# Linear attention and token/channel MLP on one core: q, k and v held as runs of nine tokens, with the head's parity on the partition halves

## The chip, the cores and the metric

The kernel runs on one core of one Trainium2 chip. The metric is the device time of one execution in microseconds (us), the median of several runs. For the kernel before it is 371.67 us (12 runs, 370.39 to 373.3).

## The reference

Inputs are q, k, v of shape (batch 8, heads 8, tokens 576, head width 64), all fp32, and the weights of a token-mixing and a channel MLP.

```python
kv  = einsum('bhsd,bhse->bhde', k, v)          # 64 x 64 for each batch and head
out = einsum('bhsd,bhde->bhse', q, kv)
x   = out / sqrt(mean(out*out, -1) + 1e-6) * g_norm   # heads side by side: (8, 576, 512)
tok = einsum('ts,bsd->btd', w_tok, alpha1*x + beta1)  # w_tok is 576 x 576
u   = x + lam * tok
ch  = relu((alpha2*u + beta2) @ w_ch1) @ w_ch2        # 512 -> 2048 -> 512
result = u + lam * ch                                 # fp32
```

## The kernel before, in words

**A recorded program and a planner.** The kernel does not issue instructions as it is written. `P.op` records an operation with its engine (or a choice of engines), an estimated cost and the keys it reads and writes. `schedule` then lays all operations out in time by those costs, and so fixes the order of each engine's instructions and the PSUM banks; `synchronize` sets the semaphores. On the chip each engine runs its list strictly in the order thus fixed. On SP's queue the early loads have a hand-written order (`order`, line 1059). Before the first channel matmuls of batch 0 the planner fills TensorE's idle time with throw-away matmuls on zeros ("warm", line 1304).

**Layout of q, k, v.** One load (line 494) brings tokens 0 to 511 of one of q, k, v for a batch: four consecutive tokens on each of 128 partitions, for all heads, in pieces of 1024 bytes. Tokens 512 to 575 come by a second load (line 504), one token on each of 64 partitions, in pieces of 256 bytes. The loads of batch 0 are cut in two halves of four heads.

**k^T v** (`kv_groups`, line 589). For each head five matmuls in fp32 accumulate over the token chunks, four chunks of 128 tokens and the tail (its other 64 partitions are zeros, memset at line 1091). Output is 64 x 64; two heads go to the two column halves of the TensorE array (tiles of 128 rows by 64 columns). Each such fp32 matmul stands as two weight loads and two matmuls in the trace, so a batch has 80 of each.

**q times kv.** Batches 0 and 1 take q transposed by TensorE (`qt_groups`, lines 551 and 556) as fp32r: two token chunks lie under each other in 128 partitions (`qtr`), and `kvr` is block-diagonal (line 675; line 680 for the tail). Batches 2 to 7 split q into two bf16 parts (`split_q`, line 529), transpose them by DMA (`qt_dma`, line 536, five transposes of 128 x 1024 elements a batch) and multiply with a two-part bf16 `kvd` (lines 665 and 385).

**The rest.** Norm (lines 706 to 737: square on ScalarE, sums and scaling on VectorE, products with alpha1*lam*g and g on VectorE or GpSimd); token mixing (line 763, tails 776; for batch 0 in two halves, line 797); `a2b` (748) and its transpose into `a2t` (by TensorE at line 868 for batch 1, by DMA at line 860 later; line 829 for batch 0); the first channel matmul with ReLU (898 for even batches, 913 for odd ones, 929 for the first piece of batch 0, eviction at 887 and 888); the second channel matmul (963), the residual add (974) and the store (977, tails 981). Tail tokens of an even and an odd batch share one 128-partition tile.

**The order of the batches.** While batch b runs its channel matmuls, batch b+1 does q times kv and the token mixing, and batch b+2 is loaded, split, transposed, and has its k^T v done among the last matmuls of line 963. Weights w_tok, w_ch1 and w_ch2 are loaded once, between the loads of batches 0 and 1, and cast (w_tok: `wt_groups`, transposes at 1121 and 1138; w_ch1 at 1217; w_ch2 at 1230 and 1235).

Of the kernel before, what the change touches and what calls it, by code (L numbers as in the profile page):

```python
# [14 lines left out]
NH = 8  # L15
S = 576
DH = 64
# [374 lines left out]
def bass_transnormer_attn__then__resmlp_affine_kernel(  # L392
# [15 lines left out]
    with ExitStack() as stack:  # L408
# [5 lines left out]
        with nc.sbuf_tensor("qtr", [128, 20, 128], F32R) as qtr:  # L414
            pass
        qs = sb("qs", [128, 5, NH, 2, DH], BF16)
# [12 lines left out]
        kf = sb("kf", [128, NH, 4, DH], F32)  # L429
        vf = sb("vf", [128, NH, 4, DH], F32)  # L430
        qf = sb("qf", [128, NH, 4, DH], F32)
        kft = sb("kft", [128, NH, DH], F32)
        qft = sb("qft", [128, NH, DH], F32)
        vft = sb("vft", [128, NH, DH], F32)
        with nc.sbuf_tensor("kvr", [128, NH, 128], F32R) as kvr:
            pass
        qt = sb("qt", [128, NH, TP], BF16)
# [54 lines left out]
        def load_main(n, b, hs, at=None):  # L492
            tile, src = {"k": (kf, k), "v": (vf, v), "q": (qf, q)}[n]
            P.op("SP", 0.6, lambda e: e.dma_start(  # L494
                tile[:, hs].rearrange("p h c d -> p h (c d)"),
                src[b, hs, 0:512, :].rearrange("h (p c) d -> p h (c d)", c=4)),
                w=[(n + "f", a) for a in halves(hs)],
                dma_us=3.0 * (hs.stop - hs.start) / 8, at=at,
                slack=0.0 if at is not None else SLACK)

        def load_tail(n, b, hs=ALL[0], at=None):
            tile, src, lo, key = {"k": (kft, k, 0, "kft"), "v": (vft, v, 0, "vft"),
                                  "q": (qft, q, 64 * (b % 2), "qft%d" % (b % 2))}[n]
            P.op("SP", 0.7, lambda e: e.dma_start(  # L504
                tile[lo:lo + 64, hs, :], src[b, hs, 512:576, :].rearrange("h s d -> s h d")),
                w=[(key, a) for a in halves(hs)], dma_us=1.2 * (hs.stop - hs.start) / 8,
                at=at, slack=0.0 if at is not None else SLACK)

        def load_kv(b, at=None):
            for n in "kv":  # L510
                load_main(n, b, ALL[0], at and at(n))
                load_tail(n, b, ALL[0], at and at(n + "t"))

        def load_q(b, at=None):
            load_main("q", b, ALL[0], at and at("q"))
            load_tail("q", b, ALL[0], at and at("qt"))

        def split_q(b):

            lo_, par = 64 * (b % 2), b % 2  # L520
            for c in range(5):
                rows = slice(0, 128) if c < 4 else slice(lo_, lo_ + 64)
                src = qf[:, :, c, :] if c < 4 else qft[rows]
                hi, lo = qs[rows, c, :, 0, :], qs[rows, c, :, 1, :]
                kin = [("qf", 0), ("qf", 1)] if c < 4 else [("qft%d" % par, a) for a in range(2)]
                kh, kl = ((("qs", c, i) if c < 4 else ("qs", c, par, i)) for i in range(2))
                P.op("ACT", act_us(512), lambda e, hi=hi, src=src: copy(e, hi, src),
                     r=kin, w=[kh])
                P.op(dve_pool(512), 0, lambda e, hi=hi, lo=lo, src=src: e.tensor_tensor(  # L529
                    out=lo, in0=src, in1=hi, op=ALU.subtract), r=kin + [kh], w=[kl], port=True)  # L530

        def qt_dma(b):
            for c in range(5):
                keys = ([("qs", c, i) for i in range(2)] if c < 4 else
                        [("qs", c, par, i) for par in range(2) for i in range(2)])
                P.op("SP", 1.3, lambda e, c=c: e.dma_start_transpose(
                    qt[:, :, 128 * c:128 * c + 128],
                    qs[:, c].rearrange("p h i d -> p (h i d)")), r=keys, w=[("qt", c)],
                    dma_us=0.8, slack=SLACK)

        def qt_groups(b):

            def group(a, cp):
                t = P.ptile(1)
                lo = 64 * (b % 2)
                n = 512 if cp < 2 else 128

                def f(e):
                    for i in range(4 if cp < 2 else 2):
                        if cp < 2:  # L550
                            m = e.transpose(t.flat()[:, 128 * i:128 * i + 128],
                                            qf[:, 4 * a + i, 2 * cp:2 * cp + 2, :].rearrange(
                                                "p c d -> p (c d)"), ident[:])
                        else:
                            h = 4 * a + 2 * i
                            m = e.transpose(t.flat()[:, 64 * i:64 * i + 64],
                                            flat(qft[lo:lo + 64, h:h + 2, :]),
                                            ident[lo:lo + 64, lo:lo + 64])
                    return m
                P.op("PE", 0.131 * (4 if cp < 2 else 2), f, cold=True,  # L560
                     r=["ident", ("qf", a) if cp < 2 else ("qft%d" % (b % 2), a)], w=[t])
                if cp < 2:
                    o = qtr[:, 8 * cp + 4 * a:8 * cp + 4 * a + 4, :].rearrange("p h s -> p (h s)")
                    s = lambda: t.flat()
                else:
                    o = qtr[:, 16 + 2 * a:18 + 2 * a, lo:lo + 64]
                    s = lambda: t.flat()[:, 0:128].rearrange("p (h s) -> p h s", h=2)
                P.op(act_dve(n) if b else "ACT", act_us(n), lambda e: copy(e, o, s()),
                     r=[t], w=[("qtr", a, cp)])
            for a in range(2):  # L570
                for cp in range(3):
                    yield lambda a=a, cp=cp: group(a, cp)

        def kv_groups(b, parts=ALL):
            def group(hs):
                t = P.ptile(1)
                h0, np_ = hs.start, (hs.stop - hs.start) // 2
                aa = halves(hs)

                def mm(prs):  # L580
                    def f(e):
                        for pr in prs:
                            for c in range(5):
                                for y in range(2):
                                    h = h0 + 2 * pr + y
                                    o = t.flat(slice(64 * y, 64 * y + 64))[:, 64 * pr:64 * pr + 64]
                                    a, w = ((kf[:, h, c], vf[:, h, c]) if c < 4 else
                                            (kft[:, h], vft[:, h]))
                                    m = e.matmul(o, a, w, start=(c == 0), stop=(c == 4),  # L589
                                                 tile_position=(0, 64 * y))  # L590
                        return m
                    P.op("PE", 0.2 + 0.585 * len(prs), f, cold=True, w=[t, ("kvp", hs.start)],
                         r=[("kf", a) for a in aa] + [("vf", a) for a in aa] + [
                             (n, a) for n in ("kft", "vft") for a in aa] + ["kv0"])
                mm(range(np_))

                def src(h):
                    return t.flat(slice(64 * h, 64 * h + 64))[:, 0:64 * np_].rearrange(
                        "p (x y) -> p x y", y=64)
                if b < R32:  # L600
                    prev = {}
                    for k_, (hp, r_) in enumerate(((0, 0), (1, 0), (1, 1), (0, 1))):
                        o = kvr[64 * r_:64 * r_ + 64, h0 + hp:hs.stop:2,
                                64 * r_:64 * r_ + 64]
                        prev[hp] = [P.op(
                            "ACT" if k_ % 2 == 0 else "DVE",
                            act_us(64 * np_) if k_ % 2 == 0 else dve_us(64 * np_),
                            lambda e, o=o, hp=hp: copy(e, o, src(hp)), hold=[t],
                            r=[("kvp", hs.start), "kvz"], w=[("kvr", a, hp, r_) for a in aa],
                            after=prev.get(hp, []))]  # L610
                    return
                kv5 = kvd[:].rearrange("p (x h) i d -> p x h i d", h=2)
                for h in range(2):
                    for r_ in range(2):
                        hi = kv5[64 * r_:64 * r_ + 64, :, h, 0]
                        P.op("ACT", act_us(256), lambda e, h=h, hi=hi: e.activation(  # L616
                            hi, src(h), ACT.Identity), r=[t], w=[("kvd", h, r_, 0)])
                for h in range(2):
                    for r_ in range(2):
                        rows = slice(64 * r_, 64 * r_ + 64)  # L620
# [720 lines left out]
```

## Time and profile before

| What | Value |
|---|---|
| median of 12 runs | 371.67 us |
| the profiled execution | 373.3 us, of which 371.5 us span from first to last instruction |
| TensorE matmuls busy | 358.3 us, 96% of the span |
| VectorE, ScalarE, GpSimd busy | 57%, 39%, 31% |
| granted TensorE clock, mean | 0.995 |
| DMA | 59.89 MB in 94626 packets, mean 161 GB/s |

Times of the page are in us unless marked ns. PE is TensorE's matmuls, PEld its weight loads, DVE is VectorE, ACT ScalarE, POOL GpSimd, SP SyncE, which issues most DMAs ("SPq"). A row of the groups names line, engine, operation, output<-inputs, shapes and count, then busy time and mean ns of one, then the idle time of the engine before them and what ended it. "busy" of matmuls includes their pipeline, so overlapping ones count once. The chain of waits is followed back from the last instruction.

### The profile page before, as it was taken

To read this page: it belongs to the slowest core of one execution; us is meant where nothing else is said; L and a number is where in the kernel's file an instruction comes from. 1 tells how busy PE (TensorE), PEld (TensorE's weight loads), DVE (VectorE), ACT (ScalarE), POOL (GpSimd) and SP (SyncE) were. 2 spreads that over 40 slices of the span, in tenths; PEclk is the share of its full clock that TensorE was granted. 3 is DMA by queue.
4 is the path that set the end of the run, shared out by engine and by line. 5 is a ranking of instruction groups with operands and counts; after the bars stand their busy time and mean duration, and the time that the engine had idled before them with its cause. 6 is when DMAs were issued, how large, how long until landed. Compare 5 with 4: busy or idle time off the path is not lost.

```text
span 371.5 us, 6839 instructions
## 1 busy us (share of the span) xinstructions
PE 358.3 (96%) x2994; PEld 215.2 (58%) x2787; DVE 210.7 (57%) x315; ACT 145.4 (39%) x250; POOL 115.7 (31%) x91
## 2 busy tenths in 40 slices
PE   8989889999999999999999999999999999999996
PEld 6867557447764465347764564447754554447644
DVE  3446558986388259852867159753854179720021
ACT  1667326226763058104761048306630057007600
POOL 4259115661076006710554003820531004400000
PEclk9999989999999999999999999999999999999999
DMA  7999999809993999269992779146915110230022
GB/s 203 283 346 276 296 328 321 205 19 170 253 241 70 220 284 226 59 136 267 226 196 43 241 210 215 42 115 172 226 29 114 58 30 0 58 99 30 0 58 85
DMA packets 94626, 59.89 MB, mean 161 GB/s; under 512 B 60592, under 2 KB 85444, under 8 KB 94596
## 3 DMA queue, kind: packets, MB, share of 16 engines
q1 hardware_dynamic: 94512, 59.44, 65.8%
q8 instruction: 23, 0.38, 0.4%
q14 instruction: 7, 0.06, 0.0%
q10 hardware_dynamic: 84, 0.02, 0.0%
HBM read 38.60 MB, written 9.44 MB: 129 GB/s over the span
## 4 chain that ended last, share of the span: by engine, by line
PE 82%; DMA 7%; SPq 4%; DVE 3%; POOL 2%; issue 1%; ACT 0%; POOLq 0%; DVEq 0%
PE ps L963 32%; PE ps L913 19%; PE ps L898 12%; PE ps L763 8%; PE ps L589 4%; DMA stg<-in_moe_w_ch_dram 4%; DMA g_bc<-in_g_norm_dram 3%; PE ps L665 2%; PE ps L385 2%; SPq L504 2%; PE ps L776 1%; SPq L494 1%; POOL xm L737 1%; PE ps L675 1%; DVE w L1235 1%
## 5 line engine op out<-in xcount | busy, mean ns | idle before, releaser
L963 PE MATMUL ps<-w,ht 128*128 128x512 bf16 (+1 forms) x569 | 125.8, 373 | 2.0 <-issue 1.1
L963 PEld LDWEIGHTS ps<-w,ht 128*128 128x128 bf16 x592 | 56.8, 98 | 64.4 <-issue 1.2
L887 ACT ACTIVATE ht<-ps,bias 128x640 bf16<-128x640 f32 (+2 forms) x98 | 72.2, 739 | 52.0 <-PE ps L913 39.9
L913 PE MATMUL ps<-a2t,w 128*128 128x320 bf16 x512 | 71.8, 299 | 0.0
L913 PEld LDWEIGHTS ps<-a2t,w 128*128 128x128 bf16 x512 | 49.4, 98 | 19.9
L737 POOL TENSOR_TENSOR xm<-xm,g_bc 128x1024 f32<-128x1024 f32 (+1 forms) x16 | 34.6, 2161 | 68.6 <-DVE rt L734 64.4
L898 PE MATMUL ps<-a2t,w 128*128 128x512 bf16 x231 | 53.8, 381 | 0.8 <-issue 0.3
L974 DVE TENSOR_TENSOR xm<-ps,xm 128x512 f32<-128x512 f32 (+1 forms) x33 | 22.2, 673 | 53.7 <-PE ps L963 53.6
L616 ACT ACTIVATE kvd<-ps 64x256 bf16<-64x256 f32 x24 | 9.1, 378 | 97.9 <-PE ps L589 97.7
L898 PEld LDWEIGHTS ps<-a2t,w 128*128 128x128 bf16 x240 | 22.6, 98 | 25.6 <-issue 0.6
L888 DVE TENSOR_SCALAR ht<-ps,bias 128x512 bf16<-128x512 f32 (+2 forms) x34 | 25.2, 750 | 16.5 <-PE ps L913 9.7
L708 DVE TENSOR_REDUCE small<-sq 128x16 f32<-128x1024 f32 (+3 forms) x27 | 24.9, 931 | 12.8 <-ACT sq L706 12.5
L763 PE MATMUL ps<-rt,wt 128*128 128x512 bf16 x140 | 31.4, 379 | 0.8 <-DVE rt L734 0.8
L529 POOL TENSOR_TENSOR qs<-qf,qs 128x512 bf16<-128x512 f32 x13 | 16.1, 1236 | 46.3 <-ACT qs L481 45.8
L734 POOL TENSOR_TENSOR rt<-xm,e_bc 128x1024 bf16<-128x1024 f32 (+1 forms) x9 | 16.9, 1875 | 41.8 <-DVE xm L730 39.8
L746 DVE TENSOR_TENSOR xm<-ps,xm 128x512 f32<-128x512 f32 x28 | 19.1, 689 | 12.2 <-PE ps L763 11.8
L706 ACT ACTIVATE sq<-ps 128x1024 f32<-128x1024 f32 (+3 forms) x27 | 21.4, 797 | 11.4 <-PE ps L385 8.2
L763 PEld LDWEIGHTS ps<-rt,wt 128*128 128x128 bf16 x140 | 13.6, 98 | 17.6 <-DVE rt L734 1.3
L974 DVE TENSOR_TENSOR xtl<-ps,xtl 128x512 f32<-128x512 f32 x4 | 2.8, 690 | 36.2 <-PE ps L963 36.2
L589 PE MATMUL ps<-vf,kf 128*64 128x64 f32 x512 | 21.4, 235 | 0.7 <-DMA vft<-in_v_dram 0.7
L589 PEld LDWEIGHTS ps<-vf,kf 128*64 128x64 f32 x512 | 19.2, 148 | 3.8 <-issue 2.5
L730 DVE TENSOR_TENSOR xm<-ps,small 128x1024 f32<-128x1024 f32 (+1 forms) x18 | 19.8, 1098 | 0.3
(102 smaller groups left out, 357.7 us busy)
## 6 DMA issues: line engine op xcount, KB each, us to landing
stg<-in_moe_w_ch_dram SPq DMA_DIRECT2D x8, 1024.0 KB, 12.1
out_dram<-xm SPq DMA_DIRECT2D x31, 256.0 KB, 2.5
kf<-in_k_dram SPq DMA_DIRECT2D x7, 1024.0 KB, 8.5
vf<-in_v_dram SPq DMA_DIRECT2D x7, 1024.0 KB, 12.6
qf<-in_q_dram SPq DMA_DIRECT2D x7, 1024.0 KB, 8.0
ht<-in_moe_w_tok_dram SPq DMA_DIRECT2D x2, 576.0 KB, 8.8
kf<-in_k_dram SPq DMA_DIRECT2D x2, 512.0 KB, 6.1
vf<-in_v_dram SPq DMA_DIRECT2D x2, 512.0 KB, 8.8
```

The lines of the kernel that those rows point to most:

```text
L589: m = e.matmul(o, a, w, start=(c == 0), stop=(c == 4), tile_position=(0, 64 * y))
L706: P.op("ACT", act_us(64 * m), lambda e: e.activation(sqv, raw(), ACT.Square), r=[t], w=[("sq", sqs)])
L708: P.op("DVE", dve_us(64 * m), lambda e: e.tensor_reduce(out=smv, in_=sqv, axis=AX.X, op=ALU.add), r=[("sq", sqs)], w=[("sm", sms)], pri=-20)
L730: P.op("DVE", dve_us(64 * m), lambda e: e.tensor_tensor(out=x3, in0=raw(True), in1=inv(), op=ALU.mult), r=[t, ("sm", sms)], w=xk, pri=-200)
L737: P.op(dve_pool(64 * m) if b < 2 else "POOL", pool_us(64 * m), lambda e: e.tensor_tensor(out=x3, in0=x3, in1=gb, op=ALU.mult), r=xk + ["g" ...
L763: m = e.matmul(t.flat(), wt[:, sc if sc < 4 else 4 + b % 2, 128 * c:128 * c + 128], rt[:, rs(b, sc), :], start=(sc == 0), stop=(sc == 4))
L887: return e.activation(dst, src(), ACT.Relu, bias=bi)
L888: return e.tensor_scalar(out=dst, in0=src(), scalar1=bi, scalar2=0.0, op0=ALU.add, op1=ALU.max)
L898: m = e.matmul(t.flat(), w1[:, dj, 128 * fj:128 * fj + 128], a2t[:, dj, 0:512], start=(dj == 0), stop=(dj == 3))
L913: m = e.matmul(t.ap()[:, i, 0:320], w1[:, dj, 128 * fj:128 * fj + 128], a2t[:, dj, 320 * i:320 * i + 320], start=(dj == 0), stop=(dj == 3))
L963: m = e.matmul(t.flat()[:, 0:m_], ht[:, fj, 128 * c:128 * c + 128], w2[:, fj, lo:hi], start=(fj == 0), stop=(fj == 15))
L974: P.op("DVE", dve_us(m_), lambda e: e.tensor_tensor(out=x, in0=t.flat()[:, 0:m_], in1=x, op=ALU.add), r=[t] + keys, w=keys)
```

## The change

**Layout.** A batch of q, k or v comes in one load. Token 9s+c of a head lies on partition s of a half (s from 0 to 63), and the head's parity chooses the half: even heads on partitions 0 to 63, odd ones on 64 to 127. One piece is 9 tokens, 2304 bytes. No tail loads, tail tiles and memsets of tail tiles are left. "Chunks" of 128 tokens are now two of the nine residues c; the ninth residue is the tail.

**k^T v** runs in tiles of 64 rows by 64 columns: nine fp32 matmuls a head, 72 a batch instead of 40, dealt in turn to the four quarters of the array. Its output takes two PSUM banks, one for each row half.

**q times kv** of batches 0 and 1 uses row tiles of 64: `qtr` holds one residue on each half, `kvr` has no zero blocks and stands on both halves. 32 matmuls of one half each, and 8 tail matmuls, a batch. PSUM takes two banks for two chunks. The order of chunk pairs is (0,2), (1,3), (tail).

**q for batches 2 to 7**: the split has four operations of 512 and one of 256 elements a partition, and the DMA transposes are four of 64 partitions x 2048 elements and two of 64 x 512.

**Stores** of a 128-token chunk go out as two DMAs of 64 rows, nine tokens apart. **w_tok** is loaded with rows strided to match (five DMAs of 2304-byte rows instead of three), and permuted while being cast and evicted (more, smaller and strided operations). The broadcast of alpha1*lam*g (line 1019 before) is moved behind the first k^T v.

The core of the diff:

```diff
-        def load_main(n, b, hs, at=None):
+        def load(n, b, hs, at=None):
             P.op("SP", 0.6, lambda e: e.dma_start(
-                tile[:, hs].rearrange("p h c d -> p h (c d)"),
-                src[b, hs, 0:512, :].rearrange("h (p c) d -> p h (c d)", c=4)),
+                tile[:, hs.start // 2:hs.stop // 2].rearrange("p x c d -> p x (c d)"),
+                src[b, hs].rearrange("(x y) (s c) d -> (y s) x (c d)", y=2, c=9)),
...
-        def load_tail(n, b, hs=ALL[0], at=None):
...
-            for c in range(5):
-                P.op("SP", 1.3, lambda e, c=c: e.dma_start_transpose(
-                    qt[:, :, 128 * c:128 * c + 128],
-                    qs[:, c].rearrange("p h i d -> p (h i d)")), r=keys, w=[("qt", c)],
-                    dma_us=0.8, slack=SLACK)
+            for a in range(3):
+                for y in range(2):
+                    rows = slice(64 * y, 64 * y + 64)
+                    if a < 2:
+                        o = qt[:, y, 2 * a:2 * a + 2].rearrange("p x c s -> p (x c) s")
+                        i_ = qs[rows, 2 * a:2 * a + 2].rearrange("p x c i d -> p (x c i d)")
+                    else:
+                        o = qtt[:].rearrange("p (x y) s -> p x y s", y=2)[:, :, y, lo:lo + 64]
+                        i_ = qst[rows].rearrange("p x i d -> p (x i d)")
+                    P.op("SP", 1.3, lambda e, o=o, i_=i_: e.dma_start_transpose(o, i_),
...
-                            for c in range(5):
-                                for y in range(2):
-                                    o = t.flat(slice(64 * y, 64 * y + 64))[:, 64 * pr:64 * pr + 64]
-                                    m = e.matmul(o, a, w, start=(c == 0), stop=(c == 4),
-                                                 tile_position=(0, 64 * y))
+                        for c in range(9):
+                            for i in range(2):
+                                for y in range(2):
+                                    x = h0 // 2 + 2 * x_ + i
+                                    rows = slice(64 * y, 64 * y + 64)
+                                    m = e.matmul(
+                                        t.ap(slice(64 * i, 64 * i + 64))[
+                                            :, y, 64 * x_:64 * x_ + 64],
+                                        kf[rows, x, c], vf[rows, x, c], start=(c == 0),
+                                        stop=(c == 8), tile_position=(64 * y, 64 * i))
-                    P.op("PE", 0.2 + 0.585 * len(prs), f, cold=True, w=[t, ("kvp", hs.start)],
+                    P.op("PE", 0.2 + 1.06 * np_, f, cold=True, w=[t, ("kvp", hs.start)],
...
                 def f32(e):
-                                mm = e.matmul(o[:, x, h, :], qtr[:, 4 * cs[0] + h0 + h, :],
-                                              kvr[:, h0 + h, y], start=True, stop=True)
+                    for h in range(h0, hs.stop):
+                        for i in range(nc_):
+                            r_ = slice(64 * i, 64 * i + 64)
+                            w = (qtr[r_, h, 2 * cs[0]:2 * cs[0] + 2, :].rearrange(
+                                "p k s -> p (k s)") if nc_ > 1 else qtrt[r_, h, :])
+                            mm = e.matmul(t.ap()[:, i, 64 * (h - h0):64 * (h - h0) + 64], w,
+                                          kvr[r_, h, :], start=True, stop=True)
...
                 if c < 4:
-                    P.op("SP", 0.6, lambda e: e.dma_start(out[b, c:512:4, lo:hi], x), r=keys,
-                         dma_us=0.8)
+                    for j in range(2):
+                        n_ = 4 * (c % 2) + 2 * j + c // 2
+                        P.op("SP", 0.6, lambda e, j=j, n_=n_: e.dma_start(
+                            out[b, n_:576:9, lo:hi], x[64 * j:64 * j + 64]), r=keys, dma_us=0.6)
...
-            P.op("PE", 0.9, f, r=["ident", "e1r"], w=[te], at=-2000.0)
+            yield
+            P.op("PE", 0.9, f, r=["ident", "e1r"], w=[te], after=P.lastw[("kvp", 0)])
...
-        order = ["k0", "kt0", "v0", "vt0", "q0", "qt0", "k1", "kt1", "t0", "t1", "t2", "v1", "vt1",
-                 "q1", "qt1", "w0", "g", "w1", "w2", "Bk", "Bkt", "Bvt", "Bv", "w3", "lam", "a2", "w4", "Bqt",
+        order = ["k0", "v0", "q0", "k1", "t0", "t1", "t2", "v1",
+                 "q1", "w0", "g", "w1", "w2", "Bk", "Bv", "w3", "lam", "a2", "w4",
                  "Bq", "w5", "w6", "w7"]
```

The order of TensorE's instructions in the built program of the changed kernel differs little from that of before after batch 1. For instance, beside the first channel matmuls of batches 1 and 3 the q times kv of the next batch (lines 665 and 385) stands in blocks of 64 and 16 matmuls instead of 32, 32 and 16, and the token mixing of batch 3 (line 763) stands behind 20 matmuls of line 963 instead of 16.

## Prediction

> **What bounds the kernel now.** I read the page's shares first, then the chain of waits, then the busy times by stretch, then single groups.
>
> ```profile
> span 371.5 us, 6839 instructions
> PE 358.3 (96%) x2994; PEld 215.2 (58%) x2787; DVE 210.7 (57%) x315; ACT 145.4 (39%) x250; POOL 115.7 (31%) x91
> DMA  7999999809993999269992779146915110230022
> PE 82%; DMA 7%; SPq 4%; DVE 3%; POOL 2%; issue 1%; ACT 0%; POOLq 0%; DVEq 0%
> ```
>
> TensorE is the bound of the whole, and the DMA row says where it isn't alone: seven slices of nine tenths at the start (a slice is 9.3 us), hardly any at the end. The stretches show this as two regimes.
>
> ```profile
> 35.00:45.00 10.00, 8.54 (x86) 6.16 (x87) 7.36 (x17) 3.65 (x8) 3.04 (x6) 1.00 1.04 284
> 45.00:56.00 11.00, 8.83 (x121) 6.32 (x123) 5.40 (x10) 2.07 (x5) 1.98 (x2) 0.84 1.08 332
> 66.00:371.50 305.50, 299.06 (x2426) 170.11 (x2213) 173.39 (x235) 113.44 (x183) 87.23 (x51) 1.00 0.58 133
> ```
>
> Columns: stretch, its length, busy PE, PEld, DVE, ACT, POOL, granted clock, DMA share, GB/s. Up to about 56 us DMA is full (1.04, 1.08) and PE idles; in 45 to 56 its clock also fell to 0.84 of full. After 66 us PE is busy 299.06 of 305.5 us and DMA has room.
>
> ```profile
> 37.27 13.40 DMA stg<-in_moe_w_ch_dram
> 50.69 2.97 DVE w L1235 x3
> ...
> 57.92 1.71 PE ps L675 x16
> 60.51 1.71 PE ps L675 x16
> 62.22 0.89 PE ps L680 x8
> 85.41 2.48 PE ps L589 x80
> ```
>
> These pieces of the chain say the same: a weight load behind the full DMA queue ends the start, and from 55.8 us on nearly every piece is PE. So two things count: how soon the loads of batches 0 and 1 are through, and PE's time after 56 us, one for one.
>
> **The change, part by part.** The profiled execution took 373.3 us (371.5 of span, 1.8 around it), 1.6 above the median of 371.67. I sum differences against it and take them off the median.
>
> *q times kv of batch 1.* On the path it costs 1.71 + 1.71 + 0.89 = 4.31 us, 107 to 111 ns a matmul, although 64 columns in bf16 (line 665) pass in some 29 ns. The weight load paces it: each of these has its own of 128 fp32 columns. In the new form 32 of the 40 load only 64 rows each, halves taking turns. If both halves load at once, the 32 cost 16 x 107 = 1.71 instead of 3.42, a gain of 1.7; if not, nothing. The nearest row for concurrency is line 776, whose two column halves run together (10 matmuls of 512 columns in 1.20 us, 120 ns each, where a lone one takes 216). I take 1.6. Batch 0's are before the bound and count nothing; their cover is the wait for the second half's loads.
>
> *k^T v.* Now 40 fp32 matmuls (80 records) take 2.48 us, 62 ns a matmul with two tiles. The groups and the timeline:
>
> ```profile
> L589 PE MATMUL ps<-vf,kf 128*64 128x64 f32 x512 | 21.4, 235 | 0.7 <-DMA vft<-in_v_dram 0.7
> 85.34 0.69 PE L589 MATMUL ps<-vf,kf 128*64 128x64 f32 x16
> 85.85 0.29 PE L589 MATMUL ps<-vft,kft 128*64 128x64 f32 x4
> L1182 PE MATMUL ps<-b2hl,w 128*128 128x2 bf16 x64 | 2.2, 164 | 1.7 <-POOL w L482 1.7
> ```
>
> Sixteen records start in 0.51 us, 32 ns each on average. The single starts are finer: 85.337, 85.343, 85.443, 85.450, 85.502, 85.508, 85.560, 85.567: pairs 6 to 7 ns apart, one pair per 58 ns, for 40 pairs from first to last. While the clock was at half speed (batch 0's first half, 9.5 to 11.3 us) a pair took 106.6 ns. The first two records being 6 ns apart, they cannot be the two passes of one tile, which elsewhere (line 1019, 213 ns apart for 128 columns) follow each other by their whole length. So the two tiles run in step. With four tiles, 72 matmuls make 144 records, 36 quads. A quad costs 58 ns if nothing else binds, 58 + 2 x 6 = 70 if the stagger adds up: 36 x 58 = 2.1 to 36 x 70 = 2.5, plus 0.15 of tail, 2.25 to 2.65. I take 2.4, a gain of 0.1 in each of 7 batches on the path: 0.6.
>
> The Trainium skill speaks against this. "TensorE: Matmul & The Clock Gate", section "Back-to-back issue gap", gives a floor of about 25 ns from one matmul's start to the next, however few columns. Line 1182, two columns, agrees for one tile: 16 take 0.54 us. By that rule 144 records cost at least 144 x 25 = 3.6 us, 1.26 more with the tail than now, 8.8 us in 7 batches. The row has pairs 6 ns apart, so the floor is not one of issue for different tiles; but on average no stretch here issues faster than 12.5 ns an instruction (weight load and matmul in 25 ns), and quads at 65 ns need 8. I side with the row, and keep 3.6 as a bound.
>
> *Loads.* DMA packet records in the first 60 us: 1024 bytes 63 ns, 256 bytes 20 to 28 ns, 2048 bytes 94 to 100 ns, 2304 bytes 135 ns (only 64 of these, in a crowd). One tensor of one batch now is 1024 x 63 + 512 x 24 = 76.8 us of one engine, 4.8 us over 16. New: 512 packets at 106 (the 2048 rate scaled) to 135 ns, 3.4 to 4.3 us. Gain 0.5 to 1.4, taken 0.75. w_tok goes from 4608-byte packets (256 x 232 ns and 64 x 135 ns, 4.2 us) to 576 of the above, 3.8 to 4.9: taken as 0.4 lost. By the fourth w_ch1 piece the queue has saved 5 tensors x 0.75 - 0.4 = 3.3 us. What PE can regain is its idling: start-to-start gaps beyond the work at 33.0 (0.75), 43.4 (1.7), 50.4 (0.8), 53.5 (0.6) and the half clock from 47.0 to 50.4 (1.7): 5.5 us. Ahead of it lies POOL, 8.40 of 9 us busy in 26 to 35 us, whose product with g starts when `g_bc` lands at 25.42; that load is 3 x 0.75 - 0.4 = 1.9 earlier in the queue. w_tok's casts and evictions grow by some eight small operations of about 0.3 us on three engines, hidden under the wait for the second half's loads (v lands at 20.0, q at 22.3); uncovered they would cost 1 us. I take 2.7 of the 3.3; ends 0 and 5.
>
> *Small ones.* Batch 1's tail transposes are 4 of 109 ns instead of 4 of about 55: +0.2. The wait of token mixing on DVE at 152 us (about 1 us) gets four more matmuls (0.86) ahead of it: -0.5; ends 0 and -1. The last store is two issues, 0.385 each: +0.4, since nothing hides it. In other batches the 8 or 10 stores and 6 transposes on SP cost nothing: SP waits 71.6 us in all for DVE's residual adds there. Queued behind them are the a2t transposes, which land 7 to 11 us before use. The ACT and DVE splits of q shrink by one half-operation, off the path.
>
> *Crossbar transposes.* No row has 64 partitions. Four of the same 256 KB as now plus two small ones; if packets are halved the DMA time goes from 256-byte to 128-byte packets, at most twice. Only batch 2 is exposed: its last transpose lands at 95.0 and its first use is at 97.4. All four are now needed for the first use; a doubled time would stall some 3 us once. I take 0, since the q load is earlier too.
>
> Sum: -1.6 - 0.6 - 2.7 + 0.2 - 0.5 + 0.4 = -4.8. Against 373.3 that is 368.5; on the median 371.67 - 4.8 = 366.9.
>
> **The rivals.**
>
> *Forecast (0.56):* as summed. Its own range is 363 to 370, from the ends of the loads and k^T v.
>
> *Four tiles don't run four wide (slower, 0.22).* The array takes the instructions such that only two records are ever in flight, for instance because the two passes of one head stand next to each other in program order. Then a matmul costs 58 ns whatever its rows: 72 x 58 + 0.15 = 4.35 us, +1.87 a batch, +13.1 in seven. With the rest at -4.2, that is 380.5. In favour: before, 40 matmuls at 58 ns also give 2.34; against: the first pair of each group. It decides from k^T v of 3.1 us on, where 7 x 0.6 eats the other gains of 4.2.
>
> *The issue floor holds (0.12).* k^T v near 3.2 to 3.6: +5 to +8.8 and -4.2: 372.5 to 376.
>
> *The loads' gain is swallowed (0.10).* Startup hangs on POOL and the casts, packets of 2304 bytes take 135 ns and more, or batch 2 stalls on its transposes; PE still gains 2: 369.5 to 373.
>
> **How the numbers follow.** A measurement of this kernel tells about 0.3%, 1.1 us, from no change. The forecast is faster nearly throughout; the swallowed case is faster by half, the same or slower by the rest; the floor and the two-wide case are slower. Faster 0.60, within 0.3% 0.08, slower 0.32. The range runs from 362.5 (the forecast's lower end) to 376 (the floor's end) and leaves the two-wide case out. The likeliest is 366.9.
>
> **What would show it.** k^T v: the busy of its group per batch in the chain, 2.25 to 2.65 us for 144 records; above 3.1 the forecast is wrong. q times kv of batch 1: near 2.6 us instead of 4.31. Loads: `g_bc` landing near 23.5 instead of 25.42, the first matmul of line 929's successor near 34.4 instead of 36.1, the last transposes of batch 1's q near 54.5 instead of 57.3, PEclk above 0.84 in the stretch 45 to 56. Batch 2's first q times kv without a gap before it. Wrong altogether if DVE or POOL waits appear on the chain after 66 us.

## The result, and the profile after

The changed kernel takes 368.49 us (median of 12 runs, 367.35 to 369.92) against 371.27 before (49 runs, 370.07 to 374.26). The ratio is 0.9919, 95% interval 0.9902 to 0.9937: 3.0 us faster by the ratio, 2.8 by the medians. The forecast was 4.8. The sum was made against a profiled execution of 373.3; the profiled execution after took 368.35. That pair differs by 5.0, but the execution before lay 2.0 above its median, so the agreement of that pair with 4.8 is partly luck. Executions more than 1.5% above the fastest of their kernel are left out of every time and ratio below.

The first view is the page: span, shares, the granted clock and the DMA row in 40 slices, the chain by engine.

```profile
span 366.5 us, 7884 instructions
PE 351.8 (96%) x3509; PEld 209.2 (57%) x3302; DVE 204.0 (56%) x305; ACT 146.7 (40%) x254; POOL 121.6 (33%) x100
PEclk9989989999999999999999999999999999999999
DMA  8998996009874669378937794569945710341023
PE 92%; ACT 2%; issue 2%; DMA 1%; ACTq 0%; DVE 0%
```

PE's busy time fell by 6.5 us (358.3 to 351.8), the span by 5.0. Of the chain, PE holds 92% instead of 82% and DMA 1% instead of 7%: no weight load ends the start any more. "issue", time in which an engine waited for nothing that the profile shows, rose from 1% to 2%. The stretches say where (length, busy PE, PEld, DVE, ACT, POOL, granted clock, DMA share, GB/s):

```profile
35.00:45.00 10.00, 9.89 (x217) 7.53 (x214) 7.29 (x15) 3.01 (x6) 2.89 (x4) 1.00 0.97 334
45.00:56.00 11.00, 7.18 (x54) 5.26 (x55) 4.40 (x7) 2.71 (x6) 8.37 (x7) 0.84 1.04 381
56.00:66.00 10.00, 9.79 (x64) 5.33 (x64) 9.84 (x13) 8.24 (x15) 4.24 (x3) 1.00 0.45 166
66.00:366.50 300.50, 294.89 (x2797) 167.48 (x2584) 165.06 (x225) 111.92 (x181) 82.92 (x52) 1.00 0.54 127
```

35 to 45 us is now filled (9.89 against 8.54). But 45 to 56 is worse than before: 7.18 us of work where 8.83 stood, with the clock again at 0.84, although DMA is no longer full after 56 us (0.45 from 56 to 66 us, 1.09 before). The chain shows what stands there (start, length, what):

```profile
35.06 3.52 PE ps L932 x32
38.62 3.40 PE ps L901 x15
42.02 0.78 PE ps L1211 x32
42.80 2.13 PE ps L590 x135
44.94 3.55 issue
48.49 0.58 PE ps L590 x9
```

In the middle of batch 1's k^T v, with 135 of its 144 records done, TensorE stops for 3.55 us and then does the other nine. There is no semaphore between them: the 72 matmuls are one operation with its waits ahead. The other engines stand too: from 45 to 47 us no DVE, ACT or POOL instruction runs. DVE and ACT wait for TensorE to 49.1 us, GpSimd for a weight load to 47.16. The clock is at half speed from 48.4 to 51.8 us.

The rows of the two matmul changes, from the chain:

```profile
55.30 1.90 PE ps L680 x32
58.17 1.00 PE ps L680 x8
82.65 2.26 PE ps L590 x144
147.47 2.54 PE ps L966 x11
150.01 4.32 PE ps L766 x20
```

q times kv of batch 1 takes 1.90 + 1.00 = 2.90 us (4.31 before), k^T v 2.26 (2.48 before). Token mixing at 150 us follows the matmuls ahead of it at once. Before, it waited there for the norm on DVE:

```profile
150.44 2.64 DVE rt L734
153.09 0.05 issue
153.13 4.49 PE ps L763 x20
```

### The profile page after: what moved, and what is told of

Same layout as the page of the kernel before. It is cut to its first block, busy times and chain, and to the rows that moved or that the text cites. A ratio compares the mean times of both kernels' runs of the same rounds, so it can differ in the third digit from the quotient of the medians.

```text
span 366.5 us, 7884 instructions
## 1 busy us (share of the span) xinstructions
PE 351.8 (96%) x3509; PEld 209.2 (57%) x3302; DVE 204.0 (56%) x305; ACT 146.7 (40%) x254; POOL 121.6 (33%) x100
## 4 chain that ended last, share of the span: by engine, by line
PE 92%; ACT 2%; issue 2%; DMA 1%; ACTq 0%; DVE 0%
PE ps L966 34%; PE ps L916 19%; PE ps L901 14%; PE ps L766 8%; PE ps L590 5%; PE ps L385 2%; PE ps L670 2%; PE ps L680 2%; PE ps L800 1%; DMA w<-in_moe_beta_dram 1%; PE ps L779 1%; PE ps L1333 1%; PE ps L932 1%; PE ps L558 1%; PE ps L1188 1%
## 5 line engine op out<-in xcount | busy, mean ns | idle before, releaser
L966 PE MATMUL ps<-w,ht 128*128 128x512 bf16 (+1 forms) x569 | 126.1, 373 | 1.9 <-issue 1.0
L890 ACT ACTIVATE ht<-ps,bias 128x640 bf16<-128x640 f32 (+2 forms) x101 | 74.9, 744 | 51.3 <-PE ps L916 37.6
L966 PEld LDWEIGHTS ps<-w,ht 128*128 128x128 bf16 x592 | 56.6, 98 | 64.5 <-issue 1.6
L740 POOL TENSOR_TENSOR xm<-xm,g_bc 128x1024 f32<-128x1024 f32 (+1 forms) x16 | 33.3, 2083 | 109.0 <-DVE rt L737 108.6
L901 PE MATMUL ps<-a2t,w 128*128 128x512 bf16 x231 | 54.0, 383 | 0.9 <-issue 0.5
L901 PEld LDWEIGHTS ps<-a2t,w 128*128 128x128 bf16 x240 | 22.7, 98 | 25.4 <-issue 0.5
L766 PE MATMUL ps<-rt,wt 128*128 128x512 bf16 x140 | 31.4, 379 | 0.0
L891 DVE TENSOR_SCALAR ht<-ps,bias 128x512 bf16<-128x512 f32 (+2 forms) x31 | 22.2, 724 | 12.4 <-PE ps L901 6.3
L590 PE MATMUL ps<-vf,kf 64*64 64x64 f32 x1152 | 19.9, 225 | 3.6 <-issue 3.5
L766 PEld LDWEIGHTS ps<-rt,wt 128*128 128x128 bf16 x140 | 13.7, 98 | 16.5
L977 DVE TENSOR_TENSOR xtl<-ps,xtl 128x512 f32<-128x512 f32 x4 | 2.8, 691 | 35.5 <-PE ps L966 35.5
L590 PEld LDWEIGHTS ps<-vf,kf 64*64 64x64 f32 x1152 | 18.5, 140 | 6.9 <-issue 6.6
L751 POOL TENSOR_TENSOR a2b<-xm,a_bc 128x512 bf16<-128x512 f32 x12 | 18.2, 1513 | 9.4 <-DVE xm L749 8.9
```

What stands on the lines that cost most here:

```text
L590: m = e.matmul(t.ap(slice(64 * i, 64 * i + 64))[:, y, 64 * x_:64 * x_ + 64], kf[rows, x, c], vf[rows, x, c], start=(c == 0), stop=(c == 8) ...
L740: P.op(dve_pool(64 * m) if b < 2 else "POOL", pool_us(64 * m), lambda e: e.tensor_tensor(out=x3, in0=x3, in1=gb, op=ALU.mult), r=xk + ["g" ...
L766: m = e.matmul(t.flat(), wt[:, sc if sc < 4 else 4 + b % 2, 128 * c:128 * c + 128], rt[:, rs(b, sc), :], start=(sc == 0), stop=(sc == 4))
L890: return e.activation(dst, src(), ACT.Relu, bias=bi)
L891: return e.tensor_scalar(out=dst, in0=src(), scalar1=bi, scalar2=0.0, op0=ALU.add, op1=ALU.max)
L901: m = e.matmul(t.flat(), w1[:, dj, 128 * fj:128 * fj + 128], a2t[:, dj, 0:512], start=(dj == 0), stop=(dj == 3))
```

## The experiments

Two theories. **Theory 1**: the missing gain is the 3.55 us gap and the half clock after it, and the gap is an instruction fetch. Among the DMA packets there are some that carry instructions, 16384 bytes each, on a queue of their own (q8). They go with TensorE's count: 27 packets for its 6811 matmuls and weight loads, 23 for 5781 before, some 252 to a packet. One ran from 45.98 to 47.10 us, inside the gap; TensorE went on 1.4 us after its end. The change had made this stretch denser: 32 bias matmuls and 135 k^T v records, with their weight loads, in 2.9 us. **Theory 2**: the startup swallows the earlier loads. `g_bc` lands at 20.21 us (25.42 before), but the first channel-mixing matmul starts only 1.2 us earlier. The reason would be the casts, evictions and the late broadcast of e1 (alpha1*lam*g): ACT and DVE are busy for 10.45 and 10.29 of 12 us from 14 to 26 us, GpSimd for 8.34 of 9 from 26 to 35.

**Batch 1's k^T v put later.** `P.bias` adds to the number by which the planner orders operations: what is recorded under a bias of 85 counts as recorded 85 operations later.

```
-        run([kv_groups(1), qt_groups(1)])
+        P.bias = 85
+        run([kv_groups(1)])
+        P.bias = 0
+        run([qt_groups(1)])
```

> The changed kernel with one difference: batch 1's k^T v is put about three channel-mixing groups later in TensorE's order, out of the place right behind the bias products. Theory 1 (the gain that is missing went into the 3.55 us in which TensorE stood still inside this k^T v, because 72 dense 64x64 products followed 32 dense bias products faster than its instructions arrived through full DMA queues, and into the half clock after it): the gap at 44.9 us is gone or much smaller, granted clock in 45 to 56 us rises from 0.84, the time falls by 3 to 5 us to about 364 to 365.5, ratio to before near 0.983. Theory 2 (the gain of the earlier loads was swallowed in the startup by the casts, the late broadcast of e1 and GpSimd; the gap is a wait that something else would end as late): less than 1 us from the changed kernel's 368.5, ratio near 0.992.

Measured: 363.56 us (362.86 to 364.23), ratio 0.9796 [0.9767, 0.9825]; by this ratio and that of the changed kernel 1.2% faster than it. The chain at the new place, behind matmuls of L901, and the stretch that was at 7.18:

```profile
47.42 2.26 PE ps L590 x144
```

```profile
45.00:56.00 11.00, 10.84 (x216) 7.78 (x214) 9.96 (x13) 4.99 (x9) 9.49 (x7) 1.00 1.05 385
```

All 144 records in one piece, 10.84 of 11 us busy, clock 1.00, with DMA as full as it was (1.05). Theory 1's numbers came, the time a little below its 364 to 365.5.

**Is it the reordering itself?** The same edit in the kernel before, twice: with 75 the k^T v stays in its place and only what is around it moves, with 95 it stands behind 20 matmuls of L898.

```
-        run([kv_groups(1), qt_groups(1)])
+        P.bias = 95
+        run([kv_groups(1)])
+        P.bias = 0
+        run([qt_groups(1)])
```

> The kernel before with kv_groups(1) put later by 75 recorded operations, as in kv1_later (there 85). In the kernel before the scheduler then leaves batch 1's k^T v in the same place and moves only what follows it, so this shows what the mere reordering is worth. Theory 1 (kv1_later gains 5 us on the changed kernel because a gap that the change brought is taken out): this kernel is within 1.5 us of before, 370 to 372.5. Rival (any later order of the same work would have gained as much, and the gap has little to do with it): 366 to 368.

> The kernel before with batch 1's k^T v really behind channel-mixing groups on TensorE (put later by 95 recorded operations; it then stands behind 20 products of L898). Theory 1 (5 us of kv1_later come from taking out a gap that only the changed kernel has): within 1.5 us of before, 369.5 to 372.5. Rival (batch 1's k^T v stood in a bad place in the kernel before too, the reordering is worth as much there): 365.5 to 368.

Measured: 370.83 us, ratio 0.9986 [0.9968, 1.0004], and 372.32, ratio 1.0026 [1.0005, 1.0048]. In the second, what now stands ahead of the k^T v waits for the tail of q:

```profile
48.53 0.46 PE L556 MATMUL ps<-ident,qft 64*128 64x64 f32 x4 [3.15 <-DMA qft<-in_q_dram]
```

So the order by itself gains nothing in the kernel before, but neither run is a clean test: in the first the k^T v did not move, and in the second a wait that belongs to the old loads (3.15 us) may hide a gain. That the gap itself cost the time is shown by the next runs, which leave the k^T v in its place.

**Fewer records at the same place.** Batch 1 sums 5 of 9 residues (nc9 is 5 for batch 1, else 9); the other four are left out.

```
-                        for c in range(9):
+                        for c in range(nc9):
-                                        stop=(c == 8), tile_position=(64 * y, 64 * i))
+                                        stop=(c == nc9 - 1), tile_position=(64 * y, 64 * i))
```

> The changed kernel, but batch 1's k^T v sums only 5 of its 9 token residues (the other 4 are left out of batch 1's result): 40 products where 72 stood, same place. That takes about 1.0 us of TensorE work away by itself. Theory 1 (the gap in it comes from the number of instructions between one instruction fetch and the next): the 64 records less end the dense stretch before the fetched instructions run out, no gap inside the k^T v, and any gap comes later, among 512-wide products of 0.21 us each that stretch the instructions; 3 to 5 us besides the 1.0, 363 to 365. Theory 2 (the gap waits for something with its own time, data or a queue): TensorE stands still up to about 48.5 us all the same, and the time falls by 0 to 1 us, 367.5 to 368.5.

Measured: 362.85 us, ratio 0.9784 [0.9749, 0.982]. Of the 5.6 us less than the changed kernel, 1.0 is the work left out.

```profile
43.32 0.78 PE ps L1212 x32
44.10 1.32 PE ps L591 x80
45.42 0.16 issue
```

No gap there, and none like it later. So the gap was no wait for something with a time of its own.

**Sixteen matmuls more ahead of it.** The bias matmuls of the last piece are computed twice.

```
-                for fj in range(4):
+                for fj in [0, 1, 2, 3] * (2 if i == 3 else 1):
```

> The changed kernel, but the 16 bias products of the last weight piece, directly ahead of batch 1's k^T v, are computed twice (the same values again, over the first). That adds 16 products and 16 weight loads to TensorE's program and 0.2 us of work ahead of the place of the gap. Theory 1 (the gap lies where the fetched instructions end, a fixed count from the start): the gap comes earlier in the k^T v than behind its 135th record, by 16 records where every record is an instruction (behind about 119), by 32 where one instruction makes two records (behind about 103); its length stays 3 to 4 us. Rival (something inside this k^T v, its data or its bank, stops it): still behind the 135th record.

```profile
42.75 1.18 PE ps L1211 x48
43.93 1.90 PE ps L590 x119
45.83 3.30 issue
49.13 0.62 PE ps L590 x25
```

The gap came exactly 16 records earlier, behind the 119th. So its place is a count of instructions: a record of the k^T v with its weight load counts as much as a bias matmul with its own. Counted from the start of the program, the gap stands behind the 1200th of TensorE's matmuls and weight loads in this trace, in that of the changed kernel and in those of `kv_two_wide` and `q_kv_in_a_row` below, and behind the 1202nd in that of `kv1_quiet`. Time: 368.19 us, ratio 0.9909 [0.9873, 0.9944].

**The queues emptied.** The same TensorE order, but three weight loads are held until batch 1's k^T v (kv1) has ended.

```
-                    at=sp["w%d" % i])
+                    at=sp["w%d" % i], after=kv1 if i > 4 else ())
...
-        run([kv_groups(1), qt_groups(1)])
+        run([kv_groups(1)])
+        kv1 = P.lastw[("kvp", 0)]
+        run([qt_groups(1)])
```

> The changed kernel, same order on TensorE around batch 1's k^T v, but the loads of the second to fourth piece of the second channel-mixing weight (1024 KB each, issued at 33.8, 36.8 and 44.6 us) are issued only when batch 1's k^T v has ended. By the rates of the changed kernel the transfers issued up to 31.4 us are done at about 41 us, so the DMA queues are near empty at 42 to 46. Theory 1a (the instruction fetch stands behind data in full DMA queues): DMA share at 43 to 46 us under 0.3, the fetch runs before 44.9 or within 1 us of it, the gap of 3.55 us shrinks to under 1 us; the time falls by up to 4 us, 364.5 to 367, less what the later loads cost. Theory 1b (the fetch is asked for too late whatever the queues hold; only the count of dense instructions matters): a gap of 2 us or more stays.

Measured: 364.45 us, ratio 0.983 [0.9799, 0.986]. Chain, and DMA by the microsecond (last columns clock, DMA share, GB/s):

```profile
43.63 2.13 PE ps L590 x135
45.77 0.88 issue
46.65 0.38 PE ps L590 x9
```

```profile
42.00:43.00 1.00, 1.00 (x17) 0.60 (x16) 0.97 (x2) 0.11 (x1) 1.00 (x1) 1.00 1.02 382
43.00:44.00 1.00, 1.00 (x54) 0.98 (x54) 1.00 (x3) 0.58 (x1) 0.04 (x1) 1.00 0.30 108
44.00:45.00 1.00, 1.00 (x84) 1.00 (x77) 0.94 (x3) 0.00 (x0) 0.00 (x0) 1.00 0.10 29
```

The gap is at the same record and has shrunk from 3.55 to 0.88 us. The instruction packet tells the rest:

```
                 k^T v starts   packet runs      TensorE goes on
changed kernel   42.80          45.98 to 47.10   48.49
bias_twice       43.93          46.75 to 47.91   49.13
kv1_quiet        43.63          44.21 to 45.16   46.65
```

With full queues it runs 3.2 us after the k^T v starts, with empty ones 0.6: 2.6 us earlier, and the gap is 2.7 shorter. The packet itself takes about 1.0 to 1.2 us either way, and TensorE goes on 1.2 to 1.5 us after it. So both halves of the theory hold: the count of instructions sets the place, 0.9 us of the gap are left with empty queues, and the full queues made the other 2.7.

What the gap costs can be read from the first channel-mixing matmul to the end of the span, in one execution of each kernel. That leaves the scatter of the startup out:

```
                             us    stop in batch 1's k^T v
before, before_again         335.4, 334.7    none
changed kernel               331.6    3.55, then half clock
bias_twice                   330.8    3.30, no half clock
kv1_quiet                    327.7    0.88
kv1_later                    327.2    none
```

The changed kernel loses 4.4 us to `kv1_later` there, `bias_twice` 3.6, of which 0.4 is its added work (1.18 us of bias matmuls instead of 0.78). The other 0.5 us between the medians of `kv1_later` and the changed kernel (4.9) is not placed; the two profiled executions differ by 1.0 in the startup, ahead of the gap.

**Both at once.** Later and held.

> kv1_later and kv1_quiet together: batch 1's k^T v behind three channel-mixing groups, and the loads of the second weight's later pieces held until it has ended. Theory 1 (each alone takes the instruction gap out, so they don't add): 362.5 to 364.5, no better than kv1_later by more than 1 us; the held loads may bring a wait for w2 at 60 to 65 us. Rival (each took out another half of the lost time): about 359 to 360.

Measured: 370.57 us, ratio 0.9974 [0.9953, 0.9995]: 7 us worse than `kv1_later`, outside what either theory expected. The k^T v runs in one piece, 49.6 to 51.9 us, so theory 1 is not touched. But the held loads begin only then, and with the later pieces of w2, the second channel weight, so late the scheduler puts just 16 channel-mixing matmuls (L966) ahead of the next token mixing (L766), where `kv1_later` has 44. TensorE, in its fixed order, then waits from 62.9 to 66.95 us for the norm of batch 1 on DVE, and the clock is at half speed from 66.7 to 70.1:

```profile
62.27 1.22 DVE xm L733
...
64.46 1.72 DVE rt L737
66.20 0.70 DVE rt L737
```

The expectation named a wait for w2 there; a larger one, for the norm, came through the order that the late loads brought about. Some 2.4 us more are the start: the first channel-mixing matmul ran at 36.2 us, in `kv1_later` at 33.9.

**Startup: the broadcast of e1 back at the start, and the beta transposition later**, each on top of `kv1_later`.

```
-            P.op("PE", 0.9, f, r=["ident", "e1r"], w=[te], after=P.lastw[("kvp", 0)])
-            P.op(act_dve(512), 0, lambda e: copy(e, e1_bc[:], te.flat()), r=[te], w=["e1"])
+            P.op("PE", 0.9, f, r=["ident", "e1r"], w=[te], at=-2000.0)
+            P.op("DVE", 0.69, lambda e: copy(e, e1_bc[:], te.flat()), r=[te], w=["e1"],
+                 at=-2000.0)
```

```
-                 r=["ident", ("pc", 0), ("pc", 1)], w=[t])
+                 r=["ident", ("pc", 0), ("pc", 1)], w=[t], after=P.lastw[("kvp", 0)])
```

> As kv1_later, and the broadcast of e1 (4 products and its eviction on VectorE) is put back to the start of the program as in the kernel before. Theory 2 (part of the startup's gain is lost because the broadcast's eviction stands in ScalarE's and VectorE's busiest stretch, 14 to 19 us, and because TensorE waits idle to 7.7 us for the beta rows): TensorE is at work from 4.7 us, the first channel-mixing product starts at 33 us or before, against 33.9 in kv1_later, and the time falls by 0.5 to 1.5 us to 362 to 363. Rival (GpSimd's chain to 32 us sets the start): within 0.4 us of 363.6.

> As kv1_later, and the small transposition that waits for the beta rows (L1033, it holds TensorE idle to 7.7 us and so at half clock to about 11) is ordered behind the first k^T v. Theory 2 (half clock in the first products costs the startup): no TensorE idle between 3 and 9 us, first k^T v in 1.3 us and not 2.1, first channel-mixing product 0.5 to 0.9 us earlier, about 363. Rival (casts, evictions and GpSimd set the start, TensorE has slack there): within 0.4 us of 363.6.

Measured: 366.24 us (364.71 to 366.26, ratio 0.9865 [0.983, 0.99]) and 370.4 us (ratio 0.9989 [0.9964, 1.0013]). Neither is better than `kv1_later`, and both miss what either theory expected. The profile of the first, though, is of an execution of 373.06 us. In it the k^T v's evictions stand behind casts of the second weight on DVE, and q times kv waits for them to 57.6 us:

```profile
53.17 3.38 DVE w L1268 x3
...
57.02 0.43 DVE kvr L482
```

The order of these operations is the program's and so the same in all its executions, but none near 366 us was profiled, so how long this wait is there is not known, and I draw nothing on e1. In the second, the first k^T v did run sooner (6.3 to 7.6 us), but TensorE then stood for some 2 us, to 12.2, and the clock was at half speed from 12.2 to 22.4; the first channel-mixing matmul came at 38.0 us, 4 later than in `kv1_later`. The other 3 us or so were lost behind it, where the planner chose another order; they were not traced. So an earlier first k^T v does not by itself bring an earlier startup, and what sets the startup stays open.

**Width of k^T v.** The row half is the outer loop, so that neighbours alternate between two tiles.

```
-                        for c in range(9):
-                            for i in range(2):
-                                for y in range(2):
+                        for y in range(2):
+                            for c in range(9):
+                                for i in range(2):
```

> The changed kernel with the loop over the two row halves of k^T v put outermost, so that neighbouring products alternate between two 64x64 tiles (same rows, other columns) and not among four. The theory that the four tiles work in step (four starts 6 to 7 ns apart, once per 58 ns, 2.26 us a batch): two tiles at once need twice the steps, 4.2 to 4.4 us a batch, 7 batches of that 2 us more, 13 to 15 us in all on a TensorE that is the bound: 381 to 384, ratio near 1.03. Rival (the array takes fp32 products of this size at one per 15 ns whichever tile they are in, the order is nothing): 2.3 us a batch, 368 to 369.

Measured: 388.71 us, ratio 1.0469 [1.0431, 1.0507]. The chain at batch 3 (it counts 138 of the 144 records):

```profile
138.57 3.83 PE ps L590 x138
```

3.83 us where four tiles take 2.26. The starts come in steps of 58 ns in both. Here there are 63 steps: 54 of two records, and 9 of four, where the loop over the row halves turns. In the changed kernel there are 36 steps, each of four. That the turns run four wide is why it is less than the 4.2 expected. The order of the instructions is what makes them wide. Six batches after the start give 6 x 1.6 = 9.4 us; most of the rest is the startup, where the longer k^T v and a clock of 0.59 in 14 to 34 us put the first channel-mixing matmul at 43.9 us instead of 34.9, 9 us that I had not expected.

**Alternation in q times kv.** Eight heads of one row half, then eight of the other.

```
-                    for h in range(h0, hs.stop):
-                        for i in range(nc_):
+                    for i in range(nc_):
+                        for h in range(h0, hs.stop):
```

> The changed kernel with the two row halves of batch 0's and 1's q times kv not alternating: eight heads of one half, then eight of the other. The theory that the alternation let two row-tiled products overlap (32 records in 1.90 us against 4.31 for all 40 records before): batch 1's 32 records take 3.3 to 3.6 us, the time rises by 1.4 to 1.7 us to about 370, ratio near 0.996. Rival (the gain came from 64 rows of weights in place of zero-filled 128, in any order): 1.9 to 2.0 us for the 32, 368.5.

```profile
56.86 2.43 PE ps L680 x32
60.27 1.00 PE ps L680 x8
```

2.43 us where alternation takes 1.90, less than I expected (3.3 to 3.6): the single starts are 112 ns apart for the first four and the last three only, in between pairs appear in this order too. So alternation brings 0.5 of the 1.4 us; what the rest is due to was not tried. The time, 368.8 us, ratio 0.9943 [0.9922, 0.9964], is not told apart from the changed kernel's. The gap stands here too, 3.85 us behind the 135th record, with half clock from 51.3 to 54.7 us.

**A second execution of before.**

> The kernel before, a second profiled execution. The theory that the profiled execution of before lay about 2 us above its usual time by where its half-clock stretches fell: this one has a span of 369 to 370.5, and the difference sits before 90 us, in the granted clock of 0 to 26 or 45 to 56 us. Rival (it lies in many small places): rows by stage agree within 0.5 us each.

Measured: 371.94 us, span 370.1. It stands twice for batch 1's q, from 47.3 to 49.3 and from 51.2 to 53.7 us; the load landed at 53.65:

```profile
37.39 16.26 DMA qf<-in_q_dram
```

So TensorE loses 1.8 to 4.1 us between 43 and 54 us in each profile with the loads of before (start-to-start gaps less the work in them: 1.8 for a cast of w and 1.7 for q in the first one, 4.1 for q here, 1.8 in `before_later`, 3.3 in `before_later_more`), at instructions that change from one to the next. The whole difference of the two executions, 1.4 us, has arisen by the end of batch 2's k^T v (87.89 and 86.49 us), as expected; the granted clock of 45 to 56 us goes with it (0.84 and 1.00).

## Why the prediction was right in sign and 2 us too large

*q times kv of batch 1*: forecast -1.6, measured -1.4 (4.31 to 2.90). The mechanism held for the 32 (1.90 us, 1.71 forecast): the starts come in pairs 2 to 5 ns apart, one pair per 112 ns. The eight of the tail, which have no partner, start singly, 112 ns apart.

*k^T v*: forecast -0.6 in seven batches, measured 0.22 in each: 2.26 us, the lower end of 2.25 to 2.65. Starts at 82.684, .691, .697, .704, then .742: four within 20 ns, one quad per 58 ns. The stagger does not add up. In the six batches after the start that is -1.3, where the forecast has 0.1 a batch from its middle value of 2.4. Two rivals fall with it: the four tiles do run four wide, and the floor in the Trainium skill, "TensorE: Matmul & The Clock Gate", section "Back-to-back issue gap", would have made 3.6 us. Here, over four tiles, the array took a record every 15.7 ns in the mean.

*The wait of token mixing at 152 us*: gone, about -1.0 (a start-to-start gap of 1.16 us where 0.22 is work), where I took -0.5.

*Tail transposes*: +0.2 as forecast (L551, two of 0.11 us per half). *Last store*: from the last matmul to the end of the span 3.40 us before, 3.49 after: +0.1 and not +0.4. *Crossbar transposes*: no gap before batch 2's first use at 94.4 us.

These make -1.4 - 1.3 - 1.0 + 0.2 + 0.1 = -3.4. The medians differ by 2.8, so *loads*, forecast at -2.7, gave about +0.6. This is the step that failed. That the total is off by no more than 2.0 is partly luck: the other terms gave 1.3 us more than was forecast of them (-3.4 against -2.1). Its first half was right, and on the low side: the loads came through far sooner, and the waits for them and for the casts behind them between 43 and 54 us are gone (`kv1_later` still waits for q, to 43.3). `g_bc` landed 5.2 us earlier where 1.9 was forecast. The packets of 2304 bytes took 101 ns in the mean of the first 60 us, less than the 106 to 135 assumed: a tensor then costs 512 x 101 / 16, 3.2 us, 1.6 less than before and not 0.75, and w_tok costs 3.6 instead of 4.2, a gain where a loss was taken. Three such tensors and w_tok make some 5.4. With the gap taken out (`kv1_later`, -7.6 by its ratio, -6.5 to -8.7 by its interval) what is left for the loads is some -4.2 (-3.1 to -5.3), the full clock in 45 to 56 us among it, more than the 2.7 taken. What the step lacked was the next thing to be late. "POOL and the casts" was my rival for that, and it is half true: the first channel-mixing matmul starts at 36.1, 35.4, 35.6 and 34.3 us in four profiles with the loads of before, and at 34.9, 33.9, 35.8, 35.6, 36.1, 36.2 and 36.2 in seven with the new ones and the startup as the change made it. The startup gained nothing that rises above its own scatter, though that POOL and the casts hold it is not shown. But what turned the remaining -4.2 into +0.6 was a supply that no term names: TensorE's own instructions, 3.55 us of gap and the half clock after it, 4.9 us by the medians of the two kernels. The denser k^T v brought TensorE to the end of its fetched instructions (`kv1_short`) at a time when the DMA queues were full (`kv1_quiet`). That the earlier data had a part in it is likely, but no run tries it. That appears in none of my rivals.

*The reference execution*: the forecast took 5.5 us of idling and half clock from one execution of 373.3 as what PE can regain. That execution lay 2.0 above the median of 49, and the idling between 43 and 54 us is 1.8 to 4.1 us in the four profiles with the loads of before.

Open: why the startup runs at half clock in some executions (0.72 to 0.86 in 14 to 26 us in the five of those seven whose first channel-mixing matmul came after 35.5 us, 0.94 and 1.00 in the other two), and what the 1.2 to 1.5 us between the end of an instruction packet and TensorE's next start are. Neither was tried. When a gap brings the half clock is open too: gaps of 3.55 and 3.85 us were followed by 3.4 us of it, the one of 3.30 in `bias_twice` was not.

The best version is `kv1_later`, 363.56 us: 2.0% under before, 1.3% under the change as made (1.2% by the ratios). `kv1_quiet` (364.45) is not told apart from it.

## What to carry to other kernels

When a change makes a stretch of an engine denser, count its instructions and look at how full the DMA queues are then: the instructions come through them too, and a stop in mid-group with "issue" as its only reason is the sign. Such a stop is cured by placing the dense group among long instructions or by keeping the queues free for it, but not by both without asking what the held loads feed. When loads come sooner, name what is late next before the gain is booked, and take the idle time to be regained from several executions.

## What the runs showed of the hardware

- Instruction fetch can stop TensorE: packets of 16384 bytes, 0.95 to 1.23 us each in the five stops seen, and a stop of 0.88 us with idle DMA queues and 3.30 to 3.85 with full ones (2.20 in `kv_two_wide`, whose records come slower), behind the same count of instructions (the 1200th in four traces, the 1202nd in `kv1_quiet`).
- Four 64x64 fp32 tiles run in step: four starts within 20 ns, one quad per 58 ns; two tiles, one pair per 58 ns (`kv_two_wide`, and the tiles of 128 rows before).
- Two row-tiled products with 64 rows by 128 columns of fp32 weights run in step too, one pair per 112 ns, and overlap in part (2.43 us for 32 against 1.90) when they are not neighbours in the program.
- A packet of 2304 bytes took 101 ns in the mean (changed kernel, first 60 us), one of 1024 bytes 63 ns (before, first 60 us).
